# Two GpSimd sums of an even quad: from one place beside VectorE to two

## The chip, the cores and the metric

The kernel runs on one core of one Trainium2 chip. The metric is the device time of one execution in microseconds. The profile is one execution taken by the hardware profiler. In it PE is TensorE's matmuls, PEld its weight loads, DVE is VectorE, ACT is ScalarE, POOL is GpSimd and SP is SyncE, which only issues transfers. L821 is line 821 of the kernel.

## The reference, cut to what matters

A transformer block on 2048 tokens of width 512: layer norm, linear attention with learned feature maps, a residual, then layer norm, a mixture of experts, and another residual. The change lies in the mixture of experts:

```python
gates = softmax(xt @ wg)                      # 2048 x 8; the top 8 of 8 experts, so all of them
h = gelu(einsum("nd,edf->nef", xt, w1))       # 8 experts, 512 -> 1792
y = einsum("nef,efd->ned", h, w2)             # 1792 -> 512
out = einsum("ne,ned->nd", cw, y)             # weighted by the gates
```

All is fp32.

## The kernel before, in words

**Products.** Each fp32 operand is split into a high part, rounded by ACT (L63), and a low part, the rest, made by DVE (L64, or L690, L691, L700 and L721 for the weights of the first layer). One fp32 product is three matmuls: L74 low by high, L75 high by low, L76 high by high. So the L74 needs the high part of the moving operand and the L75 its low part.

**Fast multiplication.** Block products are done with a scheme that takes seven products for a 2 x 2 block matrix in place of eight, with sums and differences of the blocks ahead of and behind them. A *quad* is one such set for the first layer: 256 hidden rows of one expert on one half of the tokens (1024). There are 112 quads. Two quads make a *group* (56), and the second layer does its own seven products, m1 to m7, per group (`down`, L907 to L916). ACT copies each result from PSUM (L913), and GpSimd adds it to a sum in DRAM by a transfer (L915). In 46 groups (`JOINT`) the two quads share one of their products through a further level of the scheme (`joint`, L758 on, with matmuls at L774 to L776). It leaves two sums for each quad that the quads use later. The last two of these four are made by DVE at L798 and L799: each takes a PSUM bank and subtracts the small tile s5 in SBUF.

**A quad's end.** In `quad` the results lie in four PSUM banks, pa to pd. DVE adds the joint product to pd (L970) and to pb (L979), ACT applies the gelu in place (L813), and DVE multiplies by the gate weights and writes to SBUF (`gated`, L821). These three kinds of DVE operation read one operand from PSUM and one from SBUF.

**GpSimd's four sums.** The second layer's weights need four sums per group: m5 and m7, then m6 and m3. GpSimd makes them (L846), 128 x 512 elements each, both operands in SBUF. Each is put in the list `waiting` by `sums_later` and taken from it by `window` (L823). `window` makes one gelu, then a small DVE copy called the mark (L830, one column of the bank just treated) that must wait for this gelu. Then come two or three gate products. They are chained behind the mark by edges that only fix their order on DVE. The next sum of `waiting` gets an edge with a semaphore to the mark: it starts when the mark is done. An odd quad has two windows of two products with one sum each. An even quad has one window of three products (b11, b22, b12) with two sums, both waiting for its mark.

**Order.** `moe` (L1185 on) interleaves, for each group, the second layer's products of the group before with steps of the two quads and of the joint part. In groups with a joint part its third step (with L798 and L799) comes right ahead of the even quad's L970 step, and that ahead of the L979 step. The compiler then orders the instructions of each engine itself, within the data dependences and the edges given, so neighbours in the source need not be neighbours on an engine. Each engine works its instructions off in that order.

Of the kernel before, what the change touches and what calls it, by code (L numbers as in the profile page):

```python
# [12 lines left out]
ALU = mybir.AluOpType  # L13
AX = mybir.AxisListType

P = 128
# [6 lines left out]
def block_kernel(ctx: ExitStack, tc: tile.TileContext, x, wqkv, w_phi, wo, wg, w1, w2, out):  # L23
    nc = tc.nc
# [24 lines left out]
    def ps():  # L49
        return psum.tile([P, 512], F32, name="ps", tag="ps", bufs=4)  # L50
# [7 lines left out]
    def s2(shape=(P, 512), dtype=F32):  # L58
        return work.tile(list(shape), dtype, name="s2", tag="s2", bufs=HALF_SLOTS)
# [6 lines left out]
    def halves(v):  # L66

        return v.rearrange("p (b a) -> p a b", b=2)
# [493 lines left out]
    def fetch(h):  # L562

        got = []
        for i in range(len(USE) + 2):
            if i >= 2:
                put(h, USE[i - 2], got[i - 2])
                got[i - 2] = None
            if i < len(USE):
                r = s4([P, KH, 512])  # L570
                nc.sync.dma_start(r, later[h, USE[i]])
                got.append(r)
            if i >= 1:
                yield
# [41 lines left out]
    def load_cw(h, e):  # L616

        CW[h, e] = s4([P, 2, 512])
        a = h * HALF * P
        nc.sync.dma_start(CW[h, e].rearrange("p c t -> p (c t)"),  # L620
                          cwT[e, a:a + HALF * P].partition_broadcast(P))
# [121 lines left out]
    def prep(q):  # L743
        if q // 2 in JOINT:
            return (prep_second if q % 2 else prep_first)(q // 2)
        return prep1(q)
# [11 lines left out]
    def joint(g):  # L758

        h = quads[2 * g][0]  # L760
        th, tl = T5.pop(g)
        A = {n: (th[:, i], tl[:, i]) for i, n in enumerate(["a11", "a12", "a22", "s3", "s1", "s2", "s4"])}

        def cut(v, k, n):
            return v[:, k].rearrange("p (b a) -> p a b", b=2)[:, n * P:(n + 1) * P]

        B = {f"b{k + 1}{n + 1}": tuple(cut(v, k, n) for v in X[h, "t1"]) for k in range(KH) for n in range(2)}
        for i, n in enumerate(["t2", "t1", "t3", "t4"]):
            B[n] = tuple(halves(v[:, i]) for v in XI[h])

        def inner(out_, a, b, first=False):
            (ah, al), (bh, bl) = A[a], B[b]
            out_ = out_.rearrange("p (a b) -> p a b", b=2)
            nc.tensor.matmul(out_, al, bh, start=first, stop=False, skip_group_check=True)  # L774
            nc.tensor.matmul(out_, ah, bl, start=False, stop=False, skip_group_check=True)
            nc.tensor.matmul(out_, ah, bh, start=False, stop=True, skip_group_check=True)  # L776

        pair = [banks.popleft(), banks.popleft()]
        if pair[1] is blank[0]:
            pair.reverse()  # L780
        u = pair[0][:, :2 * P], pair[0][:, 2 * P:]
        v0 = pair[1][:, :2 * P]
        inner(u[0], "a11", "b11", True)
        inner(u[1], "s1", "t1")
        s5 = s2([P, 2 * P])
        seed(s5, u[1])
        seed(u[1], u[0])
        yield
        inner(u[1], "s2", "t2")
        inner(u[0], "a12", "b21")  # L790
        seed(v0, u[1])
        r = [s2(), s2()]
        S5[2 * g], S5[2 * g + 1] = r
        seed(r[0][:, :2 * P], u[0])
        yield
        inner(v0, "s3", "t3")
        inner(u[1], "s4", "b22")
        nc.vector.tensor_tensor(r[1][:, 2 * P:], v0, s5, op=ALU.subtract)  # L798
        nc.vector.tensor_tensor(r[0][:, 2 * P:], u[1], s5, op=ALU.subtract)  # L799
        yield  # L800
        inner(v0, "a22", "t4")
        seed(r[1][:, :2 * P], v0)
        banks.extend(pair)
        yield

    waiting = deque()
    mark = consts.tile([P, 1], F32, name="mark")

    def follow(ins, other, kind=mybir.DependencyClass.NoSync):
        tc.add_manual_dep(ins, other.name, mybir.DependencyInfo(kind, mybir.DependencyReason.DATA), reason="window")  # L810

    def gelu(src):
        nc.scalar.activation(src, src, AF.Gelu_apprx_tanh)  # L813

    def gated(q, b, src):

        h, e, f = quads[q]
        B = G.setdefault(q // 2, {})
        if b not in B:
            B[b] = s4([P, 2, 512])  # L820
        return nc.vector.tensor_tensor(B[b][:, q % 2], src, CW[h, e][:, int(b[2]) - 1], op=ALU.mult).ins  # L821

    def window(q, blocks, n=1):  # L823

        gelu(blocks[-1][1])
        if not waiting:
            for b in blocks:
                gated(q, *b)
            return
        first = last = nc.vector.tensor_copy(mark, blocks[-1][1][:, :1]).ins  # L830
        for b in blocks:
            ins = gated(q, *b)
            follow(ins, last)
            last = ins
        for _ in range(n):
            follow(waiting.popleft()().ins, first, mybir.DependencyClass.Sync)

    def sums_later(g):

# [53 lines left out]
    def product(q, a, b, p, first, last=True):  # L893
        wh, wl = W1[q][a]
        xh, xl = X[quads[q][0], b]
        for k in range(KH):
            mm3(p, (wh[:, k, :], wl[:, k, :]), (xh[:, k, :], xl[:, k, :]), first and k == 0, last and k == KH - 1)
# [20 lines left out]
    def hidden(q, b, src):  # L918

        gelu(src)  # L920
        gated(q, b, src)

    def seed(dst, src):

        nc.scalar.activation(dst, src, AF.Copy)  # L925

    def quad(q):

        w1n = begun.get(q + 1) or prep(q + 1)
        if q + 2 < NQ and quads[q + 2][:2] != quads[q + 1][:2]:  # L930
            load_cw(*quads[q + 2][:2])
        h, i = divmod(q + 2, NQ // NP)
        if i == 0 and h < NP:
            late["n"] = fetch(h)
        steps_ = iter(range(7))

        def operand():
            if h > 0 and next(steps_) in FETCH.get(i, ()):
                next(late["n"], 0)

        both = q // 2 in JOINT
        pa, pb, pc, pd = ps(), ps(), ps(), ps()
        product(q, "a11", "b11", pa, True)
        seed(pb, pa)
        next(w1n, 0)
        operand()
        yield
        if not both:
            product(q, "s1", "t1", pd, True)
            s5 = s2()  # L950
            nc.scalar.activation(s5, pd, AF.Copy)
            next(w1n, 0)
            operand()
            yield
        product(q, "s2", "t2", pb, False)
        seed(pc, pb)
        next(w1n, 0)
        operand()
        yield
        product(q, "a12", "b21", pa, False)  # L960
        gelu(pa)
        if both:
            next(w1n, 0)
        operand()
        yield
        if both:
            s5 = S5.pop(q)
        plus = ALU.subtract if both and q % 2 else ALU.add
        product(q, "s3", "t3", pc, False)
        nc.vector.tensor_tensor(pd, pc, s5, op=plus)  # L970
        if q % 2:
            window(q, [("b11", pa), ("b22", pd)])
        else:
            gelu(pd)
        next(w1n, 0)
        operand()
        yield
        product(q, "s4", "b22", pb, False)
        nc.vector.tensor_tensor(pb, pb, s5, op=plus)  # L979
        if q % 2:  # L980
            gelu(pb)
        else:
            window(q, [("b11", pa), ("b22", pd), ("b12", pb)], 2)
        next(w1n, 0)
        operand()
        yield
        product(q, "a22", "t4", pc, False)
        if q % 2:
            window(q, [("b12", pb), ("b21", pc)])
        else:  # L990
            hidden(q, "b21", pc)
        operand()
        yield
# [191 lines left out]
    def moe():  # L1185
        extra = None
        for s in range(1, NGR):
# [5 lines left out]
            for k in range(7):  # L1193
# [4 lines left out]
                if k == 0:  # L1198
                    pq = quad(2 * s), quad(2 * s + 1), joint(s) if s in JOINT else None
                    if s == GH + 1:  # L1200
                        st["t1 raw"] = s4([P, KH, 512])
                        nc.sync.dma_start(st["t1 raw"], later[1, "t1"])
                    if s in (2, GH + 2):
                        late["inner"] = put_inner(s // GH, st.pop("t1 raw"))
# [484 lines left out]
    for name in order:  # L1689
        n = len(traced)  # L1690
# [37 lines left out]
```

## Time and profile before

| | us |
|---|---|
| median of 3 runs | 2335.13 (2333.24 to 2336.43) |
| the profiled execution | 2336.21 |
| its span, first to last instruction | 2334.5 |
| PE busy in it | 2295.3 (98%) |
| DVE busy | 2156.9 (92%) |
| ACT busy | 1800.8 (77%) |
| POOL busy | 804.6 (34%) |

A row of the timeline gives the start, the length, the engine, the line, the operation with output and input, the count, and in brackets how long the engine stood idle before it and what ended that. Operations of one engine overlap slightly in these rows: a DVE operation is listed from its start until its last write has landed, and the next may start some 0.1 us before that. A matmul is listed with 0.38 us, but the next starts after about 0.215. So the distance between starts tells more than the length. Rows that say x2 or x3 merge neighbours of the same kind. The waits view sums up, for each line, how long it stood for which other line, how often, and the longest.

### The profile page before, as it was taken

The numbers are of one execution on the slowest core, as the hardware profiler recorded it, in microseconds if no ns is written. First come the engines' busy times: TensorE is split into PE (matmuls) and PEld (weight loads), VectorE is DVE, ScalarE is ACT, GpSimd is POOL, SyncE is SP. The second block draws the span as 40 slices with busy tenths as digits, with TensorE's granted clock in tenths as the row PEclk, the third lists the DMA queues.
The fourth block names the chain that finished last, engine by engine and source line by source line (L and its number), as shares of the span: only waits on it lengthen the run. The fifth ranks groups of instructions, "written<-read, shape, count | busy, mean of one in ns | idle before, by whom it ended". The sixth has DMA issues, their size and how long they took to land. (4 is left out here: it accounts for less than half of the span.)

```text
span 2334.5 us, 36577 instructions
## 1 busy us (share of the span) xinstructions
PE 2295.3 (98%) x12952; PEld 1999.2 (86%) x12952; DVE 2156.9 (92%) x3278; ACT 1800.8 (77%) x3123; POOL 804.6 (34%) x894
## 2 busy tenths in 40 slices
PE   9999999999999999999999999999999999999999
PEld 8888888888888888888888888888888888888887
DVE  7888999999999999999998899999999999999998
ACT  6655787878878778787887778787878878787784
POOL 6766122333223233332332542232333323233322
PEclk9999999999999999999999999999999999999999
DMA  3127467878878788887888898887899888788888
GB/s 114 33 62 249 172 159 150 171 152 167 163 157 172 146 168 155 180 156 156 161 165 203 195 185 159 175 157 158 178 190 212 157 177 157 157 161 161 162 170 189
DMA packets 182230, 380.00 MB, mean 163 GB/s; under 512 B 15616, under 2 KB 88960, under 8 KB 182016
## 3 DMA queue, kind: packets, MB, share of 16 engines
q0 software_dynamic: 63776, 210.79, 54.3%
q1 hardware_dynamic: 117472, 166.71, 22.4%
q8 instruction: 103, 1.69, 0.3%
q14 instruction: 79, 0.65, 0.1%
q10 hardware_dynamic: 800, 0.16, 0.0%
HBM read 162.05 MB, written 224.99 MB: 166 GB/s over the span
## 5 line engine op out<-in xcount | busy, mean ns | idle before, releaser
L64 DVE TENSOR_TENSOR s<-s,s 128x512 fp32r<-128x512 f32 (+1 forms) x793 | 760.7, 962 | 56.3 <-ACT s L63 56.0
L63 ACT ACTIVATE s<-s 128x512 fp32r<-128x512 f32 (+1 forms) x793 | 660.8, 843 | 102.3 <-DVE s L874 98.9
L75 PE MATMUL pacc<-s,s 128*128 128x512 f32 x1728 | 661.5, 383 | 26.4 <-DVE s L64 26.0
L74 PE MATMUL pacc<-s,s 128*128 128x512 f32 x1728 | 657.5, 381 | 3.6 <-ACT s L63 3.5
L76 PE MATMUL pacc<-s,s 128*128 128x512 f32 x1728 | 655.9, 380 | 0.0
L74 PE MATMUL ps<-s,s 128*128 128x512 f32 x1480 | 564.3, 381 | 1.1 <-DVE s L821 0.9
L75 PE MATMUL ps<-s,s 128*128 128x512 f32 x1480 | 561.3, 379 | 0.0
L76 PE MATMUL ps<-s,s 128*128 128x512 f32 x1480 | 560.9, 379 | 0.0
L913 ACT ACTIVATE s<-pacc 128x512 f32<-128x512 f32 x756 | 420.0, 597 | 14.5 <-PE pacc L76 11.5
L75 PEld LDWEIGHTS pacc<-s,s 128*128 128x128 f32 x1728 | 327.1, 189 | 91.7 <-DVE s L64 48.4
L813 ACT ACTIVATE ps<-ps 128x512 f32<-128x512 f32 x440 | 252.6, 585 | 191.0 <-DVE ps L970 82.3
L74 PEld LDWEIGHTS pacc<-s,s 128*128 128x128 f32 x1728 | 327.0, 189 | 51.2 <-ACT s L63 5.2
L76 PEld LDWEIGHTS pacc<-s,s 128*128 128x128 f32 x1728 | 327.2, 189 | 45.0
L915 POOL DMA_DIRECT2D acc0m<-s x189 | 162.4, 859 | 495.6 <-ACT s L913 476.1
L74 PEld LDWEIGHTS ps<-s,s 128*128 128x128 f32 x1480 | 280.3, 189 | 39.8 <-issue 1.1
L76 PEld LDWEIGHTS ps<-s,s 128*128 128x128 f32 x1480 | 279.9, 189 | 39.6
L75 PEld LDWEIGHTS ps<-s,s 128*128 128x128 f32 x1480 | 280.3, 189 | 35.7 <-DVE s L64 0.4
L915 POOL DMA_DIRECT2D acc1m<-s x175 | 150.6, 860 | 436.5 <-ACT s L913 427.7
L846 POOL TENSOR_TENSOR s<-s,s 128x512 f32<-128x512 f32 x159 | 206.5, 1299 | 228.7 <-DVE mark L830 217.1
L821 DVE TENSOR_TENSOR s<-ps,s 128x512 f32<-128x512 f32 x440 | 281.6, 680 | 0.0
L874 DVE TENSOR_TENSOR s<-s,s 128x1024 f32<-128x1024 f32 x224 | 275.3, 1229 | 0.1
L925 ACT ACTIVATE ps<-ps 128x512 f32<-128x512 f32 x226 | 132.2, 585 | 25.9 <-PE ps L76 17.6
(174 smaller groups left out, 2499.8 us busy)
## 6 DMA issues: line engine op xcount, KB each, us to landing
acc0m<-s POOLq DMA_DIRECT2D x196, 512.0 KB, 5.7
acc1m<-s POOLq DMA_DIRECT2D x184, 512.0 KB, 5.9
s<-in_B_w_dram SPq DMA_DIRECT2D x224, 256.0 KB
s<-in_B_w_dram SPq DMA_DIRECT2D x111, 512.0 KB
s<-cwT SPq DMA_DIRECT2D x16, 512.0 KB
s<-in_A_x_dram SPq DMA_DIRECT2D x16, 256.0 KB
s<-in_A_x_dram SPq DMA_DIRECT2D x8, 512.0 KB
rden<-sq SPq DMA_DIRECT2D x16, 256.0 KB
```

The costliest lines, as they stand in the source:

```text
L63: nc.scalar.activation(hi, src, AF.Copy)
L64: return eng.tensor_tensor(lo, src, hi.bitcast(F32), op=ALU.subtract)
L74: nc.tensor.matmul(out_, al, bh, start=first, stop=False, skip_group_check=True)
L75: nc.tensor.matmul(out_, ah, bl, start=False, stop=False, skip_group_check=True)
L76: nc.tensor.matmul(out_, ah, bh, start=False, stop=last, skip_group_check=True)
L813: nc.scalar.activation(src, src, AF.Gelu_apprx_tanh)
L821: return nc.vector.tensor_tensor(B[b][:, q % 2], src, CW[h, e][:, int(b[2]) - 1], op=ALU.mult).ins
L846: r = nc.gpsimd.tensor_tensor(v[m], v[a], v[b], op=op)
L874: nc.vector.tensor_tensor(r, B[a], B[b], op=ALU.subtract)
L913: nc.scalar.activation(e[:, d], p[d], AF.Copy)
L915: return nc.gpsimd.dma_start(macc[h, m], e, accum_op=ALU.add)
L925: nc.scalar.activation(dst, src, AF.Copy)
```

## The change

The first of the two sums of an even quad, in groups with a joint part, is tied to the instruction at L799 in place of the mark: a semaphore from the end of L799. The second is tied to the L979 addition. The mark of the even quad is gone: the three gate products are chained directly behind L979. In even quads without a joint part there is no L799 to use, so both sums are tied to L979. Odd quads keep their marks.

```diff
         nc.vector.tensor_tensor(r[1][:, 2 * P:], v0, s5, op=ALU.subtract)
-        nc.vector.tensor_tensor(r[0][:, 2 * P:], u[1], s5, op=ALU.subtract)
+        beside(nc.vector.tensor_tensor(r[0][:, 2 * P:], u[1], s5, op=ALU.subtract).ins)
...
+    def beside(ins):
+        if waiting:
+            follow(waiting.popleft()().ins, ins, mybir.DependencyClass.Sync)
+
-    def window(q, blocks, n=1):
+    def window(q, blocks, first=None, n=1):
 
         gelu(blocks[-1][1])
...
-        first = last = nc.vector.tensor_copy(mark, blocks[-1][1][:, :1]).ins
+        first = last = first or nc.vector.tensor_copy(mark, blocks[-1][1][:, :1]).ins
         for b in blocks:
             ins = gated(q, *b)
             follow(ins, last)
             last = ins
         for _ in range(n):
-            follow(waiting.popleft()().ins, first, mybir.DependencyClass.Sync)
+            beside(first)
...
         product(q, "s4", "b22", pb, False)
-        nc.vector.tensor_tensor(pb, pb, s5, op=plus)
+        first = nc.vector.tensor_tensor(pb, pb, s5, op=plus).ins
         if q % 2:
             gelu(pb)
         else:
-            window(q, [("b11", pa), ("b22", pd), ("b12", pb)], 2)
+            window(q, [("b11", pa), ("b22", pd), ("b12", pb)], first, 1 if both else 2)
```

## The prediction

> **What bounds the kernel now.** I read the page's busy shares first, then the list of who waited for whom on PE, then PE's timeline around one such wait, and last the timeline of DVE, ACT and POOL over the 18 us ahead of it.
>
> ```profile
> span 2334.5 us, 36577 instructions
> PE 2295.3 (98%) x12952; PEld 1999.2 (86%) x12952; DVE 2156.9 (92%) x3278; ACT 1800.8 (77%) x3123; POOL 804.6 (34%) x894
> PE pacc L75 <- DVE s L64: 26.0, 48, 0.8
> ```
>
> PE is nearly full, so a change to DVE or GpSimd can only pay where PE stands still for them. One kind of wait carries nearly all of that: 48 times PE's L75 waits for a low half that DVE makes at L64, 26.0 us in total. In order of time 44 of these are one per group of two quads where two groups with a joint part follow each other, first and last:
>
> ```profile
> 408.97 0.48 PE L75 MATMUL pacc<-s,s 128*128 128x512 f32 x1 [0.51 <-DVE s L64]
> ...
> 998.34 0.48 PE L75 MATMUL pacc<-s,s 128*128 128x512 f32 x1 [0.59 <-DVE s L64]
> 1034.03 0.38 PE L76 MATMUL ps<-s,s 128*128 128x512 f32 x1
> 1034.24 0.38 PE L74 MATMUL pacc<-s,s 128*128 128x512 f32 x1
> 1035.15 0.48 PE L75 MATMUL pacc<-s,s 128*128 128x512 f32 x1 [0.53 <-DVE s L64]
> 1035.47 0.38 PE L76 MATMUL pacc<-s,s 128*128 128x512 f32 x1
> 1035.69 0.38 PE L74 MATMUL pacc<-s,s 128*128 128x512 f32 x1
> ...
> 2225.75 0.48 PE L75 MATMUL pacc<-s,s 128*128 128x512 f32 x1 [0.54 <-DVE s L64]
> ```
>
> The true loss is read from the starts. Matmuls start every 0.215 us on average (1034.03 to 1034.24, 1035.47 to 1035.69). Here 1034.24 to 1035.47 takes 1.23 us for two steps that need 0.43: 0.80 us lost, in a group of 36.81 us (998.34 to 1035.15). Why L64 is late stands in the same group's other engines:
>
> ```profile
> 1015.95 0.68 DVE L64 TENSOR_TENSOR s<-s,s 128x512 fp32r<-128x512 f32 x1
> 1016.94 0.42 DVE L798 TENSOR_TENSOR s<-pacc,s 128x256 f32<-128x256 f32 x1 [0.31 <-PE pacc L776]
> 1017.28 1.22 DVE L64 TENSOR_TENSOR s<-s,s 128x1024 fp32r<-128x1024 f32 x1
> 1017.63 0.86 POOL L915 DMA_DIRECT2D acc0m<-s  x1 [5.13 <-ACT s L913]
> 1018.41 0.42 DVE L799 TENSOR_TENSOR s<-pacc,s 128x256 f32<-128x256 f32 x1
> 1018.93 0.70 DVE L970 TENSOR_TENSOR ps<-ps,s 128x512 f32<-128x512 f32 x1
> 1019.66 0.58 ACT L813 ACTIVATE ps<-ps 128x512 f32<-128x512 f32 x1 [1.59 <-DVE ps L970]
> 1019.86 0.70 DVE L979 TENSOR_TENSOR ps<-ps,s 128x512 f32<-128x512 f32 x1 [0.23 <-PE ps L76]
> 1020.60 0.58 ACT L813 ACTIVATE ps<-ps 128x512 f32<-128x512 f32 x1 [0.35 <-DVE ps L979]
> 1021.21 0.16 DVE L830 COPY mark<-ps 128x1 f32<-128x1 f32 x1 [0.65 <-ACT ps L813]
> 1021.32 1.89 DVE L821 TENSOR_TENSOR s<-ps,s 128x512 f32<-128x512 f32 x3
> 1021.54 2.64 POOL L846 TENSOR_TENSOR s<-s,s 128x512 f32<-128x512 f32 x2 [3.06 <-DVE mark L830]
> 1023.12 1.87 DVE L700 TENSOR_TENSOR s<-s,s 128x768 fp32r<-128x768 f32 x1
> 1024.45 0.86 POOL L915 DMA_DIRECT2D acc0m<-s  x1 [0.26 <-ACT s L913]
> 1024.92 1.21 DVE L874 TENSOR_TENSOR s<-s,s 128x1024 f32<-128x1024 f32 x1
> 1026.65 1.21 DVE L874 TENSOR_TENSOR s<-s,s 128x1024 f32<-128x1024 f32 x1
> 1027.90 1.58 ACT L63 ACTIVATE s<-s 128x1024 fp32r<-128x1024 f32 x2 [1.62 <-DVE s L874]
> 1029.00 1.23 DVE L64 TENSOR_TENSOR s<-s,s 128x1024 fp32r<-128x1024 f32 x1 [0.19 <-ACT s L63]
> 1030.56 0.58 ACT L813 ACTIVATE ps<-ps 128x512 f32<-128x512 f32 x1 [0.59 <-PE ps L76]
> 1031.05 1.08 ACT L913 ACTIVATE s<-pacc 128x512 f32<-128x512 f32 x2
> 1032.01 1.07 ACT L63 ACTIVATE s<-s 128x1024 fp32r<-128x1024 f32 x1
> 1033.67 0.29 DVE L715 TENSOR_TENSOR s<-s 128x128 f32<-128x128 f32 x1
> 1033.88 1.22 DVE L64 TENSOR_TENSOR s<-s,s 128x1024 fp32r<-128x1024 f32 x1
> ```
>
> L979 is in step with PE (it waits 0.23 us for a product). From there a chain of DVE work, with one step on ACT (L63 at 1027.90), leads almost without a gap to the L64 at 1033.88, whose end at 1035.10 lets PE go. Two things in it are not work. DVE stands 0.65 us at the mark until the gelu of pb is done. And L700 takes 1.87 us, because the second of two GpSimd sums runs until 1024.18 (1021.54 + 2.64), past the end of the three gate products. The same line in an odd quad, with no sum beside it, takes 0.94:
>
> ```profile
> 1006.00 0.94 DVE L700 TENSOR_TENSOR s<-s,s 128x768 fp32r<-128x768 f32 x1
> ...
> 1006.94 1.27 DVE L821 TENSOR_TENSOR s<-ps,s 128x512 f32<-128x512 f32 x2
> 1007.11 1.28 POOL L846 TENSOR_TENSOR s<-s 128x512 f32<-128x512 f32 x1 [3.17 <-DVE mark L830]
> 1008.14 0.80 DVE L64 TENSOR_TENSOR s<-s,s 128x512 fp32r<-128x512 f32 x1
> ```
>
> The rows of the odd window also show what does not suffer: two products that read PSUM take 1.27 us beside a sum, no more each than the three in 1.89. The next two-SBUF-input operation does suffer, 0.80 against 0.68 (the L64 at 1015.95), only for what is left of the sum.
>
> **Step 1: the first sum moves to L799.** It starts about 0.17 us after L799 ends (the mark's end at 1021.37 to the sum at 1021.54 is 0.17), so at 18.83 + 0.17 = 1019.00, and takes 1.28: to 1020.28. GpSimd is free: its L915 of 1017.63 has ended at 1018.49 and the next comes at 1024.45. Nothing on GpSimd is queued behind the new wait before 1024.45, and no SP transfer is moved past anything. Beside it DVE runs L970 and L979. No sum runs beside those two lines now, so their cost is bounded: from below zero, by the products beside a sum in the odd window (a gain has no source); from above 0.93, L700's excess. I take zero: like the products they read one operand from PSUM and one from SBUF.
>
> What speaks for that reading is the Trainium skill, "SBUF — State Buffer", section "SBUF: two separate sides": DVE and GpSimd share a port pair under an exclusive lock, which a DVE instruction needs only with two SBUF inputs or in a two-port mode, and the loser blocks until the other's instruction ends. By that rule L700 would lose from 1023.12 to 1024.18, 1.06 us, where the rows give 0.93. The change takes away either amount, and the sum goes by 0.93. The rule also gives the one way in which step 1 can hurt, below.
>
> **Step 2: the mark goes in even quads, and the products follow L979 directly.** The mark's 0.11 us (1021.21 to 1021.32) and the 0.65 ahead of it go from DVE. DVE instructions follow at 0.60 for this size (L979 with 0.70 overlaps the next by some 0.1; three products span 1.89 − 0.09 = 1.80, to L700's start). So b11 starts at 1020.46, b22 at 1021.06, b12 at 1021.66 and L700 at 1022.26. The inputs are there: the gelu of pd ends at 1020.24, that of pb at 1021.18, 0.48 ahead of b12. The gain is 1023.12 − 1022.26 = 0.86.
>
> **Step 3: the second sum waits for L979.** It starts at 1020.56 + 0.17 = 1020.73 and ends at 1022.01, 0.25 ahead of L700. So L700 falls to 0.94 and its 0.93 are gained. DVE's chain is 0.86 + 0.93 = 1.79 earlier at L874.
>
> **What of it arrives.** The second L874 would end near 1026.1 instead of 1027.86, so ACT's L63 of 1027.90 runs at about 1026.3 (ACT has stood 1.62 us for it), and the chain on DVE up to L715 is 1.6 earlier: L715 ends at 1032.3. But the last L64 also needs ACT's L63 of 1032.01, and that one is fixed by PE: it comes straight after L913 and the L813 of 1030.56, which waited for PE. From the start of such an L63 to the start of its L64 takes 1.10 (1027.90 to 1029.00). So L64 cannot start before 1033.11; that is 0.77 earlier than 1033.88, and DVE has about 0.8 us to spare there. Its result lets PE go at 1034.38, where PE's own rhythm puts L75 at 1034.46 (1034.24 + 0.215). The 1034.38 keeps the 1.27 from L64's start to PE's (1033.88 to 1035.15). **ACT's L63 is what is late next, and it is just early enough.** Of the 0.80 lost per group 0.77 come back; the other 1.0 of the chain's gain becomes idle time of DVE.
>
> The sum: 44 groups by 0.77 is 33.9 us. The few groups with shorter waits than these (around 1672 and 1706) give less, so I take 33. The 7 of the 53 even windows that lie in groups without a joint part keep both sums in one window, from L979 on; their sums overrun the products much as now, and no PE wait of the repeating kind stands there: nothing. (53 windows: 159 marks in all, of which each group has three. The changed kernel has 106.)
>
> ```profile
> L830 DVE COPY mark<-ps x159: 143/151/160, 300.7 to 2248.6; 128x1 f32<-128x1 f32 x159
> L799 DVE TENSOR_TENSOR s<-pacc,s x46: 406/418/424, 392.2 to 2245.8; 128x256 f32<-128x256 f32 x46
> ```
>
> The profiled execution took 2336.2 us, 1.7 above its span and 1.1 above the median of the runs, 2335.1. So 2303 against the former, and **2302 us** against the median.
>
> **Rivals.**
>
> *ACT or a moved instruction eats part of it.* The order of DVE's instructions is the compiler's: in the rows the x low L64 (1017.28) stands between L798 and L799, which are neighbours in the source. If L700 is now put ahead of b12, it runs beside the second sum; that costs up to 0.35 (1021.66 to 1022.01) of a chain that has 1.0 to spare, so alone it changes nothing. If ACT's L63 comes later by half of its 0.77 because ACT's own instructions are reordered, 44 by 0.38 is left: 17 us, 2318. For it: the margin to PE's rhythm is under 0.1. Against: the instructions ahead of that L63 follow PE, not DVE.
>
> *No change.* The chain would have to lose 1.8 again, for instance 0.93 at L970 or L979 beside the first sum and as much again elsewhere. One of these alone still leaves 0.86, enough. So 2335 needs two failures at once, or a wait on ACT that stands at the same place already.
>
> *Slower: the lock at the new place.* If the compiler puts a two-SBUF-input operation behind L799, and it starts after the first sum has, it is blocked to the sum's end, as L700 was at 1023.12. With the L64 of 1017.28 in that place: blocked to 1020.28, it ends near 1021.4, L970 and L979 follow at 0.60 each, and L979 ends at 1022.7 instead of 1020.56, 2.14 late. Against the chain's gain of 1.79 that is 0.35 behind now: 44 by 0.35 is 15 us, 2350. It decides from the point where that operation starts over 0.17 us after L799's end. For it: such an operation stands one place ahead now. Against: the edit changes nothing that orders DVE before L799, and if L64 only swapped with L799 it would start before the sum, which would then wait instead. The lock rule of the Trainium skill named above says the same: whoever starts first holds the ports.
>
> **How the numbers follow.** The forecast, the PE wait gone or nearly gone (2295 to 2311), gets 0.65; the partial case 0.18; no change 0.07; slower 0.10. About 0.2% (4.7 us) is what a measurement of this kernel can tell from nothing, so faster is 0.83, same 0.07, slower 0.10. The lower end is 44 whole waits of 0.80 plus a few us from the groups without a joint part: 2295. The upper end takes in most of the partial case, down to a gain of 12: 2323. That leaves out about 0.2.
>
> **What would show it.** Right: 106 marks; the wait of PE's L75 for L64 down from 26 us to under 5; groups of 36.0 to 36.2 instead of 36.81; L700 near 0.94 in both quads; the sum behind L799 within L970 and L979, which stay at 0.70; the three products directly behind L979; DVE waiting for ACT's L63 ahead of the last L64. Wrong: L970 or L979 well over 0.70 or an L64 of 2 us behind L799 (the lock), or the PE wait of 0.5 still there with ACT's L63 as its releaser.

## The result, and the profile after

| | before | after |
|---|---|---|
| median of 4 runs, us | 2335.78 (2333.24 to 2336.88) | 2293.51 (2292.85 to 2294.28) |
| span of the profiled execution, us | 2334.5 | 2292.5 |

The ratio is 0.9821 [0.9804, 0.9838]: faster, as forecast, by 42 us where 33 were forecast. 2293.5 lies 1.5 below the lower end of the range. Lines behind the edit are numbered 4 higher in the new kernel (5 in the two with a further edit at `waiting`): the sums stand at L850, the mark at L834, the two additions at L974 and L983, the weight sums on DVE at L878.

The page of the changed kernel, its row of busy times, and the row of its waits view for PE that answers to the 26.0 us of before:

```profile
PE 2280.3 (99%) x12952; PEld 2000.1 (87%) x12952; DVE 2106.2 (92%) x3225; ACT 1799.8 (79%) x3123; POOL 807.1 (35%) x894
```

```profile
PE pacc L75 <- DVE s L64: 2.1, 3, 0.8
```

The wait has gone but for 3 cases. DVE is busy for 50.7 us less, and L700 holds most of it: 131.5 us in 92 runs before (mean 1429 ns), and now, in the groups view with busy time and mean ns behind the bar, 87.1:

```profile
L700 DVE TENSOR_TENSOR s<-s,s 128x768 fp32r<-128x768 f32 x92 | 87.1, 946 | 1.7 <-DMA acc1m<-s 1.7
```

Now one group of the changed kernel, its timeline from L799 on, with the rows that answer to those of before:

```profile
1111.16 0.42 DVE L799 TENSOR_TENSOR s<-pacc,s 128x256 f32<-128x256 f32 x1
1111.68 0.70 DVE L974 TENSOR_TENSOR ps<-ps,s 128x512 f32<-128x512 f32 x1
1111.72 1.28 POOL L850 TENSOR_TENSOR s<-s,s 128x512 f32<-128x512 f32 x1 [0.49 <-DVE s L799]
1112.61 0.70 DVE L983 TENSOR_TENSOR ps<-ps,s 128x512 f32<-128x512 f32 x1 [0.23 <-PE ps L76]
1113.22 1.88 DVE L821 TENSOR_TENSOR s<-ps,s 128x512 f32<-128x512 f32 x3
1113.46 1.29 POOL L850 TENSOR_TENSOR s<-s,s 128x512 f32<-128x512 f32 x1 [0.45 <-DVE ps L983]
1115.01 0.95 DVE L700 TENSOR_TENSOR s<-s,s 128x768 fp32r<-128x768 f32 x1
1115.88 1.22 DVE L878 TENSOR_TENSOR s<-s,s 128x1024 f32<-128x1024 f32 x1
1123.52 1.07 ACT L63 ACTIVATE s<-s 128x1024 fp32r<-128x1024 f32 x1
1124.47 0.60 ACT L813 ACTIVATE ps<-ps 128x512 f32<-128x512 f32 x1
1124.90 1.22 DVE L64 TENSOR_TENSOR s<-s,s 128x1024 fp32r<-128x1024 f32 x1
1126.99 0.38 PE L74 MATMUL pacc<-s,s 128*128 128x512 f32 x1
1127.21 0.38 PE L75 MATMUL pacc<-s,s 128*128 128x512 f32 x1
```

From L983 to the first L878 now takes 3.27 us (1112.61 to 1115.88), before 5.06 (1019.86 to 1024.92): 1.79 less. L974 and L983 keep their 0.70 beside the first sum; the products follow L983 at 0.61; L700 comes after the second sum has ended (1113.46 + 1.29 = 1114.75) and takes 0.95. The last L64 starts 12.29 after L983, before 14.02: 1.73 less. And PE's L75 starts 0.22 after its L74, without a wait.

Where the 42 us come from is read by stretches between starts of L799, the line that every group with a joint part passes once: first two timeline rows of the new kernel with the view of this line, which has its first and last start (390.9 and 2204.4), then the two rows of the old kernel that are not in the prediction.

```profile
1183.14 0.41 DVE L799 TENSOR_TENSOR s<-pacc,s 128x256 f32<-128x256 f32 x1
1406.00 0.41 DVE L799 TENSOR_TENSOR s<-pacc,s 128x256 f32<-128x256 f32 x1
L799 DVE TENSOR_TENSOR s<-pacc,s x46: 411/415/424, 390.9 to 2204.4; 128x256 f32<-128x256 f32 x46
```

```profile
1202.55 0.42 DVE L799 TENSOR_TENSOR s<-pacc,s 128x256 f32<-128x256 f32 x1
1431.93 0.41 DVE L799 TENSOR_TENSOR s<-pacc,s 128x256 f32<-128x256 f32 x1
```

| stretch | before | after | gained |
|---|---|---|---|
| start to the first L799 | 392.2 | 390.9 | 1.3 |
| 22 steps of a group, joint | 810.4 | 792.2 | 18.2 |
| the middle: groups without a joint part | 229.4 | 222.9 | 6.5 |
| 22 steps of a group, joint | 813.9 | 798.4 | 15.5 |
| last L799 to the end | 88.7 | 88.1 | 0.6 |

The joint groups give 33.7, the sum of the prediction (33 to 33.9). The middle gives 6.5 that it put at nothing. They go with one event. PE of the old kernel stood still once for long, and ran at half its rate behind it. Its timeline there:

```profile
1284.66 1.73 POOL L1006 DMA_DIRECT2D acc0m<-acc0m  x2 [5.99 <-DMA acc0m<-s]
1285.24 3.55 DVE L874 TENSOR_TENSOR s<-s,s 128x1024 f32<-128x1024 f32 x1
1285.79 1.91 POOL L846 TENSOR_TENSOR s<-s,s 128x512 f32<-128x512 f32 x1
1287.78 2.15 POOL L846 TENSOR_TENSOR s<-s,s 128x512 f32<-128x512 f32 x1
1288.71 1.76 DVE L64 TENSOR_TENSOR s<-s,s 128x512 fp32r<-128x512 f32 x1
1289.85 0.38 PE L76 MATMUL ps<-s,s 128*128 128x512 f32 x1
1290.39 1.21 DVE L874 TENSOR_TENSOR s<-s,s 128x1024 f32<-128x1024 f32 x1
1291.98 1.06 ACT L63 ACTIVATE s<-s 128x1024 fp32r<-128x1024 f32 x1 [3.13 <-DVE s L874]
1293.08 1.22 PE L74 MATMUL pacc<-s,s 128*128 128x512 f32 x2 [2.86 <-ACT s L63]
1296.21 0.63 PE L76 MATMUL pacc<-s,s 128*128 128x512 f32 x1
1296.63 0.63 PE L75 MATMUL pacc<-s,s 128*128 128x512 f32 x1
1299.57 0.38 PE L76 MATMUL pacc<-s,s 128*128 128x512 f32 x1
```

Read it from PE back. L74 waits 2.86 us for ACT's L63, that one 3.13 for the L874 that ends at 1291.60. Ahead of it on DVE another L874 takes 3.55 in place of 1.21 and an L64 1.76 in place of 0.68, each beside a GpSimd sum. The two sums are there because they stand in GpSimd's queue behind a transfer (L1006) that has waited 5.99 us for another DMA. Between the L76 of 1289.85 and that of 1299.57 lie 15 matmul starts, 3.23 us at 0.215; it took 9.72. The loss is 6.5 us, as much as the middle gained. Part of it is the rate behind the stop, 0.42 from start to start (1296.21 to 1296.63). The windows view of the old kernel has the granted clock in the third column from the right:

```profile
1034.00:1036.00 2.00, 1.47 (x7) 0.96 (x7) 2.00 (x3) 2.00 (x4) 0.00 (x0) 1.00 0.84 131
...
1294.00:1296.00 2.00, 1.96 (x5) 1.39 (x5) 2.00 (x6) 1.36 (x4) 0.00 (x0) 0.50 0.74 129
```

It is 0.50 behind a stop of 3.0 us (1290.07 to 1293.08), where the stop of 0.53 us at 1035.15 in a joint group left it at 1.00. The Trainium skill, "TensorE: Matmul & The Clock Gate", Part 1, describes a gate that falls to half rate after about one window of 3.4 us without work; the half rate agrees with the 0.42. This stop was shorter than that window, and in a run below (the first mark of odd quads gone) a stop of 2.4 us was followed by a clock of 0.50 too; the measurement decides here.

In the new kernel both sums stand ahead of that transfer. Its timeline at the same place:

```profile
1260.26 3.49 POOL L850 TENSOR_TENSOR s<-s,s 128x512 f32<-128x512 f32 x2 [3.06 <-DVE ps L983]
1263.71 2.55 POOL L1010 DMA_DIRECT2D acc0m<-acc0m  x3
```

The source says nothing on the order of a sum and this transfer on GpSimd. The compiler put the sums ahead when they wait for L983 and behind when they wait for the mark.

### The profile page after: what moved, and what is told of

The parts are those of the page before. It is cut to its first block, busy times and chain, and to the rows that moved or that the text cites. A ratio compares the mean times of both kernels' runs of the same rounds, so it can differ in the third digit from the quotient of the medians.

```text
span 2292.5 us, 36624 instructions
## 1 busy us (share of the span) xinstructions
PE 2280.3 (99%) x12952; PEld 2000.1 (87%) x12952; DVE 2106.2 (92%) x3225; ACT 1799.8 (79%) x3123; POOL 807.1 (35%) x894
## 5 line engine op out<-in xcount | busy, mean ns | idle before, releaser
L64 DVE TENSOR_TENSOR s<-s,s 128x512 fp32r<-128x512 f32 (+1 forms) x793 | 762.1, 964 | 92.2 <-ACT s L63 89.9
L63 ACT ACTIVATE s<-s 128x512 fp32r<-128x512 f32 (+1 forms) x793 | 662.0, 845 | 33.2 <-DVE s L878 21.4
L75 PE MATMUL pacc<-s,s 128*128 128x512 f32 x1728 | 656.4, 380 | 2.2 <-DVE s L64 2.1
L74 PE MATMUL pacc<-s,s 128*128 128x512 f32 x1728 | 656.5, 380 | 0.3 <-DVE s L64 0.3
L76 PE MATMUL pacc<-s,s 128*128 128x512 f32 x1728 | 654.9, 379 | 0.0
L74 PE MATMUL ps<-s,s 128*128 128x512 f32 x1480 | 564.2, 381 | 1.3 <-DVE s L821 0.7
L75 PE MATMUL ps<-s,s 128*128 128x512 f32 x1480 | 561.3, 379 | 0.7 <-DVE s L64 0.7
L76 PE MATMUL ps<-s,s 128*128 128x512 f32 x1480 | 560.9, 379 | 0.0
L917 ACT ACTIVATE s<-pacc 128x512 f32<-128x512 f32 x756 | 431.0, 601 | 30.2 <-PE pacc L76 20.1
L813 ACT ACTIVATE ps<-ps 128x512 f32<-128x512 f32 x440 | 254.6, 590 | 205.9 <-DVE ps L974 81.1
L75 PEld LDWEIGHTS pacc<-s,s 128*128 128x128 f32 x1728 | 326.7, 189 | 51.9 <-DVE s L64 7.7
L74 PEld LDWEIGHTS pacc<-s,s 128*128 128x128 f32 x1728 | 326.6, 189 | 46.3 <-ACT s L63 1.0
L76 PEld LDWEIGHTS pacc<-s,s 128*128 128x128 f32 x1728 | 326.6, 189 | 45.7
L74 PEld LDWEIGHTS ps<-s,s 128*128 128x128 f32 x1480 | 280.0, 189 | 40.2 <-PE ps L76 1.5
L76 PEld LDWEIGHTS ps<-s,s 128*128 128x128 f32 x1480 | 279.7, 189 | 39.5
L75 PEld LDWEIGHTS ps<-s,s 128*128 128x128 f32 x1480 | 280.2, 189 | 36.9 <-DVE s L64 1.8
L878 DVE TENSOR_TENSOR s<-s,s 128x1024 f32<-128x1024 f32 x224 | 271.9, 1214 | 0.1
L850 POOL TENSOR_TENSOR s<-s,s 128x512 f32<-128x512 f32 x159 | 210.2, 1322 | 129.7 <-DVE mark L834 72.4
```

Source lines behind the costliest of these rows:

```text
L63: nc.scalar.activation(hi, src, AF.Copy)
L64: return eng.tensor_tensor(lo, src, hi.bitcast(F32), op=ALU.subtract)
L76: nc.tensor.matmul(out_, ah, bh, start=False, stop=last, skip_group_check=True)
L850: r = nc.gpsimd.tensor_tensor(v[m], v[a], v[b], op=op)
L878: nc.vector.tensor_tensor(r, B[a], B[b], op=ALU.subtract)
L917: nc.scalar.activation(e[:, d], p[d], AF.Copy)
```

## The experiments

The theory (A in the expectations) has two parts. In joint groups DVE was late by 0.80 a group; the change takes 1.79 from its chain, so that about 1 us is spare and PE sets the pace. In the middle the mark's absence turns the order on GpSimd, and the long stop goes. The rivals: that what the sums cost counts in proportion rather than up to a limit; that the middle's gain comes from elsewhere; that only the mark's removal, or only the parting, does the work. A group's length below is the mean of the first 22 steps of L799: 36.83 before, 36.01 in the changed kernel. The kernel before was timed again beside them: 2337.31, 2336.55 and 2337.09 in the three sets. Diffs are against the changed kernel, but for the last.

**The joint groups alone.** The window of even quads without a joint part is as before.

```diff
-            window(q, [("b11", pa), ("b22", pd), ("b12", pb)], first, 1 if both else 2)
+            window(q, [("b11", pa), ("b22", pd), ("b12", pb)], first if both else None, 1 if both else 2)
```

> The change in the groups with a joint part alone; even quads of the other groups keep the mark with both sums. Theory A (two gains: 0.80 us of PE wait in each of 44 joint groups, and one long stall near 1290 that came from the order of GpSimd's work): GpSimd's order still has the transfer of L1010 ahead of the two sums there, so groups take 36.0 us but a PE wait of about 2.9 us with a lowered clock stays once: 2300 to 2303. Rival B (the long stall went by a shift in time alone): 2293 to 2295, no such stall.

Measured 2302.02 (2301.88 to 2303.21), ratio 0.985 [0.9836, 0.9865]. A group takes 36.02; the middle takes 228.91, 0.5 less than before, and the stop is in its timeline:

```profile
1275.83 0.70 PE L74 MATMUL pacc<-s,s 128*128 128x512 f32 x2 [2.53 <-ACT s L63]
```

So the forecast of 2302 is what the joint groups alone are worth.

**The other groups alone.**

```diff
-        beside(nc.vector.tensor_tensor(r[0][:, 2 * P:], u[1], s5, op=ALU.subtract).ins)
+        nc.vector.tensor_tensor(r[0][:, 2 * P:], u[1], s5, op=ALU.subtract)
...
-            window(q, [("b11", pa), ("b22", pd), ("b12", pb)], first, 1 if both else 2)
+            window(q, [("b11", pa), ("b22", pd), ("b12", pb)], None if both else first, 2)
```

> The change in the even quads of groups without a joint part alone. Theory A: GpSimd's order has both sums ahead of the transfer of L1010; the long stall goes, joint groups stay at 36.8 us with a PE wait of 0.5 each: 2327 to 2330. Rival B: the stall stays, 2334 to 2337.

Measured 2329.78 (2327.52 to 2331.03), ratio 0.9969 [0.9957, 0.9981]. A group stays at 36.8, the middle is 223.19, and PE's longest wait in the middle is 0.8. The two parts of the change add up: medians 35.3 lower there and 7.5 here, together 42.8, where the whole change has 42.3.

**Parted, with the mark.**

```diff
-            window(q, [("b11", pa), ("b22", pd), ("b12", pb)], first, 1 if both else 2)
+            window(q, [("b11", pa), ("b22", pd), ("b12", pb)], None, 1 if both else 2)
```

> The first sum goes to L799, but the even window keeps its mark, and the second sum waits for it. Theory A (the chain needs to be only some 0.8 to 0.9 us earlier): L700 falls from 1.87 to 0.94, DVE's chain gains 0.93 and the PE wait of the joint groups falls to 0.1 or less: groups of 36.0 to 36.1; the long stall stays (the order on GpSimd is that of before): 2301 to 2306. Rival C (the gain is in proportion to what the chain gains, 0.93 of 1.79): half, about 2316 to 2319.

Measured 2302.94 (2301.8 to 2304.37), ratio 0.9854 [0.9838, 0.9871]. A group takes 36.05: the parting alone gives the joint groups nearly all of their gain, since L700's 0.93 is more than the 0.80 that was lost. Proportion is refuted. The middle (228.34) keeps its stop, so most of what the mark's removal adds lies there. In 6 of the 46 joint groups the timeline has one thing more:

```profile
1112.36 1.22 DVE L64 TENSOR_TENSOR s<-s,s 128x1024 fp32r<-128x1024 f32 x1
1112.60 2.12 POOL L850 TENSOR_TENSOR s<-s,s 128x512 f32<-128x512 f32 x1 [5.08 <-DVE s L799]
```

Here the compiler did put a two-SBUF L64 behind L799, the place of the prediction's slower rival, but it started 0.24 before the sum: L64 kept its 1.22 and the sum waited, 2.12 in place of 1.28.

**No mark, not parted.**

```diff
-        beside(nc.vector.tensor_tensor(r[0][:, 2 * P:], u[1], s5, op=ALU.subtract).ins)
+        nc.vector.tensor_tensor(r[0][:, 2 * P:], u[1], s5, op=ALU.subtract)
...
-            window(q, [("b11", pa), ("b22", pd), ("b12", pb)], first, 1 if both else 2)
+            window(q, [("b11", pa), ("b22", pd), ("b12", pb)], first, 2)
```

> The mark goes, but both sums wait for the L983 addition, one behind the other. Theory A: the sums run until about 2.8 us after L983 ends, so L700 is blocked for about 1.1 us (it takes about 2.0); the chain gains 0.7 of 1.79, the PE wait in joint groups falls to 0.1 to 0.2, groups of 36.1 to 36.2; the long stall goes: 2296 to 2302. Rival C: 0.7 of 1.79 is 40% of the gain, 2315 to 2318.

Measured 2298.79 (2297.23 to 2299.05), ratio 0.9834 [0.9819, 0.9849]. The time is as expected, and so is the blocked line: L700 takes 1.9 in 45 of the 46 joint groups. One of them:

```profile
1078.91 0.70 DVE L983 TENSOR_TENSOR ps<-ps,s 128x512 f32<-128x512 f32 x1 [0.28 <-PE ps L76]
1079.76 2.63 POOL L850 TENSOR_TENSOR s<-s,s 128x512 f32<-128x512 f32 x2 [2.22 <-DVE ps L983]
1081.31 1.90 DVE L700 TENSOR_TENSOR s<-s,s 128x768 fp32r<-128x768 f32 x1
1083.14 1.21 DVE L878 TENSOR_TENSOR s<-s,s 128x1024 f32<-128x1024 f32 x1
```

The second sum runs to 1082.39, and L700 waits for it. The chain gains 0.83 (L878 ends 5.44 after L983; before, 6.27), a little more than the 0.80 that was lost, and a group takes 36.02. In the one other group (L983 at 1114.96) L700 came in between the two sums with its usual 0.95, the second sum waited for it, and L878 waited for the sum (2.29 in place of 1.21). So in joint groups either part nearly suffices, and both together are worth no more, save as a reserve.

**The even sums left out.** m6 and m3 are not made; the blocks m1 and m2 stand in for them, so the second layer's result is another one. The edit at L799 is undone as well, since no sum is left for it.

```diff
-        if not waiting:
+        if not waiting and first is None:
...
+        A["m6"], A["m3"] = A["m1"], A["m2"]
-        for m in (("m5", "a21", "m4", ALU.add), ("m7", "m1", "a21", ALU.subtract), ("m6", "m5", "m1", ALU.subtract),
-                  ("m3", "m2", "m6", ALU.subtract)):
+        for m in (("m5", "a21", "m4", ALU.add), ("m7", "m1", "a21", ALU.subtract)):
...
+            window(q, [("b11", pa), ("b22", pd), ("b12", pb)], first, 0)
```

> Leaves out the sums m6 and m3 (m1 and m2 stand in for them), so that no GpSimd sum runs beside an even quad; no mark there either. Theory A (PE is the limit of the joint groups now, and the two sums cost nothing any more): 36.0 us per group, 2290 to 2295. Rival: the sums still cost DVE something that PE feels: 2280 to 2287.

Measured 2294.36 (2293.79 to 2295.28), ratio 0.9821 [0.9806, 0.9835]; a group takes 36.01. With the two sums placed as in the change there is nothing left to gain from them.

**Second sum behind the products**, tied to the last of them in joint groups, where it runs beside L878.

```diff
-            beside(first)
+            beside(last if len(blocks) == 3 and q // 2 in JOINT else first)
```

> As the changed kernel, but in groups with a joint part the second sum waits for the last gate product, so that two-SBUF-input work (L700, L878) follows beside it. The L64 before PE's L75 has about 0.9 to 1.0 us to spare there. Theory A (who comes first blocks the other, up to 1.28 us): DVE's chain is up to 1.28 later and 0.1 to 0.4 us of PE wait returns per joint group: 2296 to 2312. Rival (DVE is ahead of the sum each time and GpSimd waits): nothing, 2292 to 2295.

Measured 2301.94 (2300.89 to 2303.47), ratio 0.9851 [0.9835, 0.9868].

```profile
1118.69 2.31 DVE L878 TENSOR_TENSOR s<-s,s 128x1024 f32<-128x1024 f32 x1
```

1.09 us are put back on the chain and a group takes 36.12, only 0.11 more: the spare of about 1 us is there, and this uses it up. Of the 8.4 us by which the median is above that of the changed kernel, some 4.7 are these 44 steps; most of the rest lies in the few irregular groups of the second stretch (around 1700).

**Both sums behind the products**: the edit of the last kernel, and that of "no mark, not parted".

> Both even sums of the joint groups wait for the last gate product, no mark. Double the dose: theory A: up to 2.6 us of blocking against 0.9 to 1.0 to spare, so 1.2 to 1.7 us of PE wait per joint group: 2345 to 2370, slower than the kernel before. Rival (DVE ahead, GpSimd waits): 2292 to 2296.

Measured 2351.19 (2349.08 to 2354.53), ratio 1.0065 [1.005, 1.008]: slower than before. Its timeline:

```profile
1140.15 2.30 DVE L878 TENSOR_TENSOR s<-s,s 128x1024 f32<-128x1024 f32 x1
1142.38 1.76 DVE L64 TENSOR_TENSOR s<-s,s 128x512 fp32r<-128x512 f32 x1
```

PE's L75 waits for L64 again, 35.0 us in 48 cases. Two operations are blocked, 1.08 each (2.30 against 1.22, 1.76 against 0.68): 2.16 on the chain. Before it was 1.79, so 0.37 more, and a group takes 37.20 against 36.83: 0.37. The account of the joint groups holds on this side of the limit too.

One distance sums up the joint groups of all these kernels: from the start of the second addition to the start of the last L64 (the usual value of the 44 groups). What it falls short of the 14.02 of before comes off the group, until PE's own rhythm of 36.01 is reached:

| kernel | last L64 behind the second addition | group |
|---|---|---|
| both sums behind the products | 14.40 | 37.20 |
| before | 14.02 | 36.83 |
| second sum behind the products | 13.32 | 36.12 |
| parted, with the mark | 13.24 | 36.05 |
| no mark, not parted | 13.18 | 36.02 |
| the change | 12.29 | 36.01 |

**The first mark of odd quads gone too**: their first window is chained to the L974 addition.

```diff
-        nc.vector.tensor_tensor(pd, pc, s5, op=plus)
+        first = nc.vector.tensor_tensor(pd, pc, s5, op=plus).ins
...
-            window(q, [("b11", pa), ("b22", pd)])
+            window(q, [("b11", pa), ("b22", pd)], first)
```

> The same edit carried on: the first window of the odd quads loses its mark too, its sum waits for the L974 addition. Theory A (PE is the limit in the joint groups): groups stay at 36.0, only the groups without a joint part can move: 2288 to 2297. Rival (the marks cost PE time wherever they are): 0.1 to 0.2 us per group less, 2284 to 2289.

Measured 2298.65 (2296.24 to 2300.35), ratio 0.9838 [0.9823, 0.9853], a little above what was expected. A group takes 36.00, as it should with DVE having time to spare. The loss is in the middle (225.56), where PE waits 2.15 at 1258.09 for an L64 and then runs at a clock of 0.50 (1260 to 1262). That L64 has no sum beside it; what made it late for PE there was not followed. In joint groups an odd quad's L64 is blocked by a sum, which costs nothing:

```profile
1128.05 1.60 POOL L850 TENSOR_TENSOR s<-s,s 128x512 f32<-128x512 f32 x1
1128.16 2.58 DVE L64 TENSOR_TENSOR s<-s,s 128x1024 fp32r<-128x1024 f32 x1
```

The compiler put L64 between the two products, and it started 0.11 after the sum: 2.58 in place of 1.22.

**The order on GpSimd, in the old kernel.** An edge that only fixes order puts the first of these transfers behind the even sums. `made` keeps the sums as `window` takes them; the diff is against the kernel before, in `unmix`.

```diff
-                nc.gpsimd.dma_start(macc[h, a][r], macc[h, b][r], accum_op=ALU.add, max_dma_last_dim=1024)
+                dma = nc.gpsimd.dma_start(macc[h, a][r], macc[h, b][r], accum_op=ALU.add, max_dma_last_dim=1024)
+                if h == 0 and (a, b) == ("m2", "m1"):
+                    at.append(made[-3] if not at else at[0])
+                    follow(dma.ins, at[0])
```

> The kernel before with that one edge alone, no other change. Theory A: the long wait goes, the joint groups stay at 36.8 us: 2328 to 2331. Rival: 2334 to 2337.

Measured 2334.01 (2332.31 to 2336.52), ratio 0.9987 [0.9977, 0.9997]. The 2328 to 2331 expected were missed, and the time lies in the rival's range. Yet the stop is gone (longest wait of the middle 0.8) and the middle takes 225.23, 4.2 less. That is two thirds of the 6.5; 1.3 of it is lost again in the second stretch of joint groups (815.2 against 813.9). Of the 2.0 that the middle still takes beyond "the other groups alone" (223.19), most shows as the short wait of L75 for L64, 2.9 us in 4 cases against 1.3 in 2. In "the joint groups alone" and "parted, with the mark", which keep these marks too, it is 2.9 and 2.6 in 4 cases; in the changed kernel 1.4 in 2. So the rest goes with the marks; that they are its cause was not tested by itself.

**The same edge with the joint groups alone.**

> The change in the joint groups alone, marks kept elsewhere, and one more edge that only fixes an order on GpSimd: the first transfers that add up the first half's results (L1010 in the changed kernel) come behind the two sums of the even quad ahead of them. No work is left out, no wait is added. Theory A (the long PE wait comes from the sums standing behind a transfer that waits): the wait of 2.5 us and the lowered clock go without touching a mark: 2294 to 2297. Rival (the mark's idle time on DVE does it): 2301 to 2303, as in the run with the joint groups alone.

Measured 2300.76 (2298.76 to 2302.66), ratio 0.9844 [0.983, 0.9859]: the expected 2294 to 2297 were missed, and nothing is gained over the joint groups alone. The wait at the old place is down to 0.6, but another stop of its kind stands further on:

```profile
1303.24 0.81 POOL L1011 DMA_DIRECT2D acc0m<-acc0m  x1 [3.17 <-DMA acc0m<-acc0m]
1305.00 1.79 POOL L851 TENSOR_TENSOR s<-s,s 128x512 f32<-128x512 f32 x1
1306.87 1.98 POOL L851 TENSOR_TENSOR s<-s,s 128x512 f32<-128x512 f32 x1
1307.27 2.67 DVE L879 TENSOR_TENSOR s<-s,s 128x1024 f32<-128x1024 f32 x1
1309.98 1.06 ACT L63 ACTIVATE s<-s 128x1024 fp32r<-128x1024 f32 x1 [2.53 <-DVE s L879]
1311.09 0.48 PE L74 MATMUL pacc<-s,s 128*128 128x512 f32 x1 [3.02 <-ACT s L63]
```

From PE back it reads as the stop of the old kernel does: L74 waits 3.02 for ACT's L63, that one 2.53 for an L879 that takes 2.67 in place of 1.21 beside a sum, and the two even sums come late because transfers stand ahead of them on GpSimd, the first of which waited 3.17 for another DMA. The middle is 231.1. So the mechanism is seen a second time, but this run did not confirm that an edge at one transfer removes its cost; which of the transfers bites is a matter of how the queues happen to fall.

## Why the prediction came out too high

**Right.** Steps 1 to 3 came out as worked: the sum behind L799 cost L974 and L983 nothing, the chain on DVE gained 1.79 at L878, L700 fell to 0.95, 106 marks are left. The joint groups gave 33.7 us where the sum had 33 to 33.9.

**Right in size, and in its reason only for some groups.** "ACT's L63 is what is late next, and it is just early enough" took from the rows of before that L63 is fixed to PE by the L813 and L913 ahead of it. In 6 of the 44 groups of the new kernel it went just so, for instance:

```profile
1087.26 0.58 ACT L813 ACTIVATE ps<-ps 128x512 f32<-128x512 f32 x1 [0.65 <-PE ps L76]
1088.70 1.07 ACT L63 ACTIVATE s<-s 128x1024 fp32r<-128x1024 f32 x1
1089.81 1.23 DVE L64 TENSOR_TENSOR s<-s,s 128x1024 fp32r<-128x1024 f32 x1 [0.87 <-ACT s L63]
```

DVE stands 0.87 for L63, and L64 starts 13.25 behind L983, 0.77 earlier than before. In 37 others the compiler put L63 ahead of L813 (1123.52 and 1124.47 in the group shown above), the last L64 came 1.73 earlier, and its low half is ready at 1126.17 (1124.90 + 1.27, the distance from L64 to PE's start in before) for an L75 at 1127.21. There the reserve is 1.0, not under 0.1. It changed no number, because PE's own rhythm is the limit in both accounts. The thin margin on which the chance of 0.18 for the partial case rested is real where the order is the predicted one: with "parted, with the mark" L64 comes at 13.24 in all regular groups, and a group takes 36.05, some 0.04 more than PE's rhythm, not the 0.38 of that rival.

**The step that failed** is the term for the groups without a joint part: "The 7 of the 53 even windows that lie in groups without a joint part keep both sums in one window, from L979 on; their sums overrun the products much as now, and no PE wait of the repeating kind stands there: nothing." It was 6.5. The sentence looked for the repeating wait and passed over the single one: the waits view of before has another row, with the longest wait last:

```profile
PE pacc L74 <- ACT s L63: 3.5, 3, 2.9
```

Followed back, this row would have led to the two even sums, the very instructions that the change moves, standing on GpSimd behind a waiting transfer. Those are 6.5 of the 9 us by which the gain was forecast too small; 1.9 more came ahead of the first joint group and behind the last, where I did not look for single causes. The rest lies between the 33 taken and the 33.7 measured. The lower end of the range had some 5 us for the groups without a joint part; the term itself had none.

**The slower rival** came about in one group only: there an L64 behind L799 started 0.12 after the sum (1658.16 and 1658.04) and took 2.57 in place of 1.22, and PE did not wait for it. Elsewhere no two-SBUF operation behind L799 started after the sum. Its arithmetic for a joint group holds: it put a loss of 2.14 on the chain at 0.35 a group, and "both sums behind the products" put 2.16 there, at another place, and lost 0.37. That the totals agree too, 2350 and 2351.19, is luck: that kernel gained 6.3 in the middle (223.06), which the rival did not count, and lost more than 0.37 in a few irregular groups.

**Not settled:** why the compiler ordered the sums and the transfer as it did, and whether the wait of the transfer itself could be shortened; neither was tried.

## What to carry to other kernels

A repeating wait has a limit: once the engine that waited is in its own rhythm, further time taken from the other chain is reserve, so savings of 0.86 and 0.93 against a loss of 0.80 were worth 0.8 together, and about as much when only one was made. When a change moves an instruction, look up each single long wait in the old profile as well, and follow it back: it may end at the instruction that moves. In a queue that is worked off in order, short work behind a transfer that waits for a DMA comes late by that whole wait, and lands beside other work than it was placed beside.

## What the runs showed of the hardware

GpSimd's sums and DVE's two-SBUF operations wait for each other. In the joint groups the one that starts first keeps its time: an L64 that started 0.24 before the sum lost nothing (1.22) and the sum took 2.12; one that started 0.11 after the sum took 2.58. That is the rule of the Trainium skill in "SBUF — State Buffer", section "SBUF: two separate sides", and these rows agree with it.

Other rows do not fit it by the starts that they list. In the stop of the old kernel the L874 of 1285.24 starts 0.55 ahead of the sum and still takes 2.34 more than its 1.21, and in the last experiment an L64 (1304.59, 2.76 in place of 0.68) starts 0.41 ahead of the sum of 1305.00. In both places a transfer that GpSimd issues stands right ahead of the sum; whether that is the reason is open.

How long a sum that lost has to wait is open too. In the new kernel one sum takes 4.10, to 1303.91, beside three DVE operations that follow each other closely and end at 1302.76; PE waits only 0.84 behind it:

```profile
1299.81 4.10 POOL L850 TENSOR_TENSOR s<-s,s 128x512 f32<-128x512 f32 x1
```

In the last experiment one takes 4.91 in the same way. But in the stop of the old kernel the sum of 1287.78, which waited for an L874, ran ahead of the L64 that follows that L874 directly (1288.71, 1.76).

Products that read one operand from PSUM ran beside sums at their usual 0.6 to 0.7 throughout.
